# The product with wk as seven block products per batch, with the sums of its blocks streamed from memory

## The chip, the cores and the metric

The kernel runs on one core of one Trainium2 chip. The metric is the device time of one execution in microseconds; the time shown for a kernel is the median of three runs. A profile of one execution comes with it, and the views of that profile are what the prediction reads.

## The reference

Three layers follow each other over 4 batches of 576 tokens with 512 channels: a block-causal attention with 8 heads, a mixer (a token MLP of width 256 and a channel MLP of width 1536), and the layer that the change touches:

```python
x_prev = concat([zeros, x[:, :-1]], axis=1)
xk = mu_k * x + (1 - mu_k) * x_prev
xr = mu_r * x + (1 - mu_r) * x_prev
k = maximum(xk @ w_k, 0)             # w_k: 512 x 1024
v = k * k @ w_v                      # w_v: 1024 x 512
r = 1 / (1 + exp(-(xr @ w_r)))       # w_r: 512 x 512
return r * v
```

Everything is float32 outside. Inside, each operand of a product is split into a high and a low part of a shorter float format, and a product is three matmuls: high by high, high by low, low by high (`dense`, with every matmul recorded at line 214).

## The kernel before

Activations lie channel-major: 128 channels on the partitions, tokens along the free dimension. A batch is cut into two halves of T = 288 tokens, so most matmuls of the last layer are 128 x 128 weights against 128 x 288 tokens.

**Order of the work.** The kernel is not written in the order in which it runs. Each piece of work is registered with `add` (name, engine, an assumed cost, what it depends on, which buffers it takes from rings and frees); `Plan.run` then plays a list schedule over these costs, with priorities that the table `TILT` shifts by kind, and records the instructions in that order. Each engine, and SyncE's queue of DMA issues too, therefore works through a fixed list in order, and an instruction whose inputs are late holds up all that stands behind it on its engine. In the schedule, work on GpSimd and a set of VectorE kinds (`TURNS`) are never placed at the same time.

**Stages.** Attention and the token MLP come first, the channel MLP (`L`: 12 column products per tile of 460 or 464 tokens, `O`: back) follows, then the last layer. TensorE has work in all of them.

**Weights of the last layer.** They arrive as 64-bit words. While the channel MLP runs, each page of 128 x 512 is loaded into one of four staging blocks (`raw`, `rawx`), decoded to float32 in a `td` buffer by two passes on VectorE and one each on ScalarE and GpSimd (`d0` to `d3`), split into high and low (`hi`, `lo`), and written to a scratch array in memory (`pages`). When the channel MLP's own weights are done with, the pages are read back (`ld`): 8 pages of wk and 4 of wr into the 12 slots of ring `w`, those of wv into `w2a` and `w2b`; they stay there for all four batches.

**wk (`K`, before).** Per half batch and per 128 of the 1024 output columns, 12 matmuls of 288 tokens run into one PSUM bank (4 blocks of input channels x 3). ScalarE makes relu of the bank (`KR`, line 974) and VectorE multiplies it with the bank (`KS`, line 978).

**wv (`V`, before and after).** Here the seven-product scheme is in use already. Per batch the squared activations are four blocks B11, B12, B21, B22 (halves of the channels x halves of the tokens), wv is cut in 2 x 2 blocks, and seven products of blocks and of sums of blocks (T1 to T4, line 1017) take the place of eight. The sums of the blocks of wv are made once, in `block_sums` (lines 559 to 595), from pairs of decoded pages: `vs` and `vs2` on VectorE, then the new blocks `vc` and `vd` are split and written like a page. The operands are split per block on ScalarE (`VH`) and VectorE or GpSimd (`VL`, line 211). Each product has two banks of its own, and eight sums per pair of banks (`EV`, line 1038) put the results together in `u`.

**wr (`R`).** Per half batch and 128 output columns 12 matmuls; ScalarE takes the sigmoid (line 994), VectorE multiplies (`Y`, line 998) and SyncE stores 128 x 288. In the schedule `R` waits for the sixth product of `V`.

**Mixing.** xk and xr are made per half batch on ScalarE (`XA`, line 944) and VectorE (`XM`, line 949), and split in 128 x 576 pieces (`XH` line 204, `XL` line 211).

Of the kernel before, what the change touches and what calls it, by code (L numbers as in the profile page):

```python
# [48 lines left out]
TILT = {"ku": -15.8, "h1h": -1.7, "n": -5.4, "h1l": -31.5, "xh": -12.9, "xt": -0.4, "v": 0.1, "k2": 5.6, "q": 9.0, "rc": -20.7, "KH": -1.8, "KL": -2.0, "R": -4.4, "xa": 15.9, "page-v": 16.5, "O": -8.5, "V": -4.8, "Lh": 0.4, "xsh": 17.8, "U": 1.9, "C2": -3.2, "t": -23.3, "xm": -18.3, "K": -4.3, "z": 0.4, "page-c2": 6.1, "page-k": 3.0, "Ll": 4.4, "KS": -6.1, "page-c1": -1.4, "page-t1": -3.0, "xsl": 15.2, "load": 0.5, "L": -8.8, "e": 15.0, "page-r": -3.3, "pv": 0.3, "KR": -21.0, "m": 4.3, "ev": 5.9, "TS": -26.2, "vs": 4.3, "VL": -9.7, "SG": 4.8, "Y": 1.0, "spill": 19.1, "page-vc": 4.1, "page-vd": -7.8, "VH": 3.2, "s": -1.2, "vs2": 4.3, "ld": 13.7, "xl": -2.8, "wr": -5.0, "k1": -4.9, "x2s": 0.8, "x1": 3.7, "mu": -6.1, "om": 9.0, "fetch": -5.1, "page-t2": -0.0}  # L49
# [146 lines left out]
def attn_mixer_rwkv_kernel(ctx: ExitStack, tc: tile.TileContext, z, v, vl, wt1, wt2, wc1, wc2, wk, wv, wr, mu, out):  # L196
# [16 lines left out]
    def mm(o, l, r, start, stop):  # L213
        PE.matmul(o, lhsT=l, rhs=r, start=start, stop=stop)  # L214
# [21 lines left out]
    def c_mm(n):  # L236
        return max(0.108, (n + 32) / 2400)
# [13 lines left out]
    rawt = {"raw": [wp.tile([128, 512], I64, name=f"raw{k}") for k in range(2)]}  # L251
    w1h = tokp.tile([128, 5, DTOK], F32R, name="w1h")
# [231 lines left out]
    plan.ring("td", 3)  # L484
# [21 lines left out]
    def page_ops(name, src, n, room, pri, split_pri=None, gate=(), alloc=(), dense=False, late=False, slack=0.0, store=False):  # L506
# [11 lines left out]
        def pack(e):  # L518
            tl["td", name] = wp.tile([128, 2 * T], U32, tag="td", bufs=3, name="td")[:, 0:c]
            dec2(tl["raw", name], tl["td", name])  # L520

        def hi(e):
            w = room()
            copy(e, w[0], tl["td", name].bitcast(F32))
# [19 lines left out]
    PLACE.update({("v", f): 12 + f for f in range(8)})
    PLACE.update({(nm, j): 20 + 4 * k + j for k, nm in enumerate(("vc", "vd")) for j in range(4)})
    store = nc.dram_tensor("pages", (len(PLACE), 128, 1024), F32).ap()

    def put(name):
        w = tl["raw", name].bitcast(F32)
        w = w[:, 0:512] if name[0] == "vd" else w  # L550
        SP.dma_start(out=store[PLACE[name], :, 0:w.shape[1]], in_=w)


    def block_sums(j, pri):
        a_, b_ = ("v", j), ("v", j + 4)

        def ab():
            return tl["td", a_].bitcast(F32), tl["td", b_].bitcast(F32)

        def vs(e):  # L560
            a, b = ab()
            w = tl["td", ("vc", j)] = wp.tile([128, 2 * T], U32, tag="td", bufs=3, name="td").bitcast(F32)[:, 0:512]
            DVE.tensor_tensor(w[:, 0:256], a[:, 256:512], b[:, 256:512], ALU.add)
            DVE.tensor_tensor(w[:, 256:512], w[:, 0:256], a[:, 0:256], ALU.subtract)

        def vs2(e):
            a, b = ab()
            DVE.tensor_tensor(b[:, 0:256], b[:, 0:256], tl["td", ("vc", j)][:, 256:512], ALU.subtract)
            DVE.tensor_tensor(a[:, 256:512], a[:, 0:256], a[:, 256:512], ALU.subtract)

        add(("vs", j), "DVE", 0.84, [("d3",) + a_, ("d3",) + b_], vs, pri, alloc=[("td", ("td", ("vc", j)))], uses=[("td", a_), ("td", b_)])
        add(("vs2", j), "DVE", 0.84, [("vs", j), ("lo",) + b_], vs2, pri, uses=[("td", a_), ("td", b_), ("td", ("vc", j))])
        for nm, c, ring in (("vc", 512, "raw"), ("vd", 256, "rawx")):
            rk, tk = ("raw", (nm, j)), ("td", (nm, j) if nm == "vc" else b_)

            def src(nm=nm):
                return tl["td", ("vc", j)] if nm == "vc" else ab()[1][:, 0:256]

            def hi(e, nm=nm, c=c, ring=ring, src=src):
                tl["raw", (nm, j)] = rawt[ring][plan.slot[ring, ("raw", (nm, j))]]  # L580
                copy(e, tl["raw", (nm, j)].bitcast(F32R)[:, 0:c], src())

            def lo(e, nm=nm, c=c, src=src):
                w = tl["raw", (nm, j)].bitcast(F32R)
                sub(e, w[:, c:2 * c], src(), f32(w[:, 0:c]))

            add(("hi", nm, j), ("ACT", "POOL"), {"ACT": c_act(c), "POOL": c_pool1(c)}, [("vs2", j)], hi, pri + 0.1, alloc=[(ring, rk)], uses=[tk])
            add(("lo", nm, j), ("DVE", "POOL"), {"DVE": 0.14 + 0.00109 * c, "POOL": c_pool2(c)}, [("hi", nm, j)], lo, pri + 0.1, uses=[rk, tk])
            add(("wr", nm, j), "SP", c_dma(128 * 8 * c), [("lo", nm, j)], lambda e, nm=nm: put((nm, j)), pri, uses=[rk], lat=4.0)
# [116 lines left out]
    plan.ring("w", 12)  # L706
# [6 lines left out]
    pages += [("k", f) for f in range(8)] + [("r", f) for f in range(4)] + [("v", 4 * k + j) for j in range(4) for k in range(2)]  # L713
# [3 lines left out]
    def slot(tag):  # L717
        if tag == "w":
            return wp.tile([128, 2, 512], F32R, tag="w", bufs=12, name="w")
        return pools[tag].tile([128, 2, 512], F32R, tag=tag, bufs=plan.rings[tag], name="w")  # L720

    for nm, f in pages:
        tag = "w" if nm == "c1" else "w2a" if f < 4 else "w2b"
        store_ = nm not in ("c1", "c2")

        def room(nm=nm, f=f, tag=tag, store_=store_):
            if store_:
# [7 lines left out]
        if nm == "v" and f % 4:  # L735
            gate += [("hi", "vd" if f >= 4 else "vc", f % 4 - 1)]
        page_ops((nm, f), wsrc[nm][f], 512, room, when[nm] + (0.5 * f if nm != "v" else f % 4 + f // 4 * 0.5), gate=gate + before,
                 alloc=[] if store_ else [(tag, ("W", nm, f))], dense=nm != "c1" or f >= EARLY,
                 late=nm != "c1" and (f // 4 if nm == "v" else f % 2) == 1, slack=2.0 if nm == "c1" and f < EARLY else 0.0, store=store_)
        if nm == "v" and f >= 4:  # L740
            block_sums(f - 4, when[nm] + f % 4 + 0.5)

    def fetch_page(nm, f, tag):
        if nm == "vd":
            if f == 0:
                tl["vd"] = glob.tile([128, 4, S + 1], F32R, tag="u0", bufs=1, name="vd")
            SP.dma_start(out=f32(tl["vd"][:, f, 0:512]), in_=store[PLACE["vd", f], :, 0:512])
        else:
            t = tl["W", nm, f] = slot(tag)
            SP.dma_start(out=f32(t), in_=store[PLACE[nm, f]].rearrange("p (s c) -> p s c", s=2))  # L750

    back = [("k", f, "w") for f in range(8)] + [("r", f, "w") for f in range(4)] + [("v", f, "w2a") for f in range(4)]
    back += [("vc", f, "w2b") for f in range(4)] + [("v", f, "w2b") for f in range(4, 8)] + [("vd", f, "") for f in range(4)]
    for k, (nm, f, tag) in enumerate(back):
        add(("ld", nm, f), "SP", c_dma(128 * (2048 if nm == "vd" else 4096)), [("wr", nm, f)] + (["spill"] + [("ld", "vd", 0)] * (f > 0) if nm == "vd" else []),
            lambda e, nm=nm, f=f, tag=tag: fetch_page(nm, f, tag), 100.0 + k, alloc=[(tag, ("W", nm, f))] if tag else [], lat=3.0)
# [32 lines left out]
    NGF, NGR = 20, 12  # L789
    plan.ring("gf", NGF)  # L790
    plan.ring("gr", NGR)
    plan.users["raws"] = [("wr", nm, f) for nm in ("v", "vc", "vd") for f in range(8 if nm == "v" else 4)]
    for i in range(2):
        plan.users[f"xhl{i}"] = [("L", max(s for s in range(NX) if s % 2 == i), 11)]
    for i in range(5):
        f = next(f for f in range(7, 12) if (12 * (NX - 1) + f) % 5 == i)
        plan.users[f"hp{i}"] = [("O", NX - 1, f, m) for m in range(4)] if f == 11 else [("O", NX - 1, f)]
    for i in range(NGF):
        if i < 18:
            plan.held.append(("gf", i, "raws" if i < 12 else f"hp{(i - 8) // 2}"))  # L800
    for i in range(NGR):
        plan.held.append(("gr", i, f"xhl{i // 4}" if i < 8 else f"hp{(i - 8) // 2}"))
# [340 lines left out]
```

## Time and profile before

| | |
|---|---|
| time, median of 3 runs | 779.87 us (779.3 to 780.42) |
| profiled execution: its own time, its span | 780.42 us, 778.6 us |
| TensorE busy | 769.7 us, 99% of the span, 5596 matmuls |
| VectorE, ScalarE, GpSimd busy | 483.3, 367.2, 260.6 us |
| mean granted TensorE clock | 0.997 of full speed |
| DMA, over the span | 99 GB/s |

The span runs from the first to the last instruction; the run's own time is 1.8 us more. An engine's busy time is the time in which at least one of its instructions is open; instructions that follow each other directly overlap in these records, so a mean duration is longer than the step from one start to the next.

### The profile page before, as it was taken

The numbers are of one execution on the slowest core, as the hardware profiler recorded it, in microseconds if no ns is written. First come the engines' busy times: TensorE is split into PE (matmuls) and PEld (weight loads), VectorE is DVE, ScalarE is ACT, GpSimd is POOL, SyncE is SP. The second block draws the span as 40 slices with busy tenths as digits, with TensorE's granted clock in tenths as the row PEclk, the third lists the DMA queues.
The fourth block names the chain that finished last, engine by engine and source line by source line (L and its number), as shares of the span: only waits on it lengthen the run. The fifth ranks groups of instructions, "written<-read, shape, count | busy, mean of one in ns | idle before, by whom it ended". The sixth has DMA issues, their size and how long they took to land.

```text
span 778.6 us, 14728 instructions
## 1 busy us (share of the span) xinstructions
PE 769.7 (99%) x5596; PEld 716.7 (92%) x5596; DVE 483.3 (62%) x1245; ACT 367.2 (47%) x902; POOL 260.6 (33%) x352
## 2 busy tenths in 40 slices
PE   9999999999999999999999999999999999999998
PEld 7888899899989888889888888889999999999998
DVE  5898788887475566353326255125866867776782
ACT  5887876767432353141222232023546536545551
POOL 4776676766553466261242112000010010010010
PEclk9999999999999999999999999999999999999999
DMA  7443525221142444516042144447003001001001
GB/s 194 132 123 97 170 82 161 84 89 40 56 122 94 136 136 162 189 55 250 28 162 98 65 162 159 153 168 279 1 8 115 1 1 62 2 1 62 1 1 61
DMA packets 37079, 77.11 MB, mean 99 GB/s; under 512 B 13840, under 2 KB 17936, under 8 KB 37008
## 3 DMA queue, kind: packets, MB, share of 16 engines
q1 hardware_dynamic: 37008, 76.17, 29.4%
q8 instruction: 44, 0.72, 0.4%
q14 instruction: 27, 0.22, 0.1%
HBM read 56.63 MB, written 19.53 MB: 98 GB/s over the span
## 4 chain that ended last, share of the span: by engine, by line
PE 97%; DVE 1%; POOL 0%; ACT 0%; issue 0%; ACTq 0%
PE b L214 69%; PE cd L214 22%; PE b L389 4%; PE b L391 1%; PE b L618 1%; POOL P L380 0%; DVE xnh L206 0%; DVE xnl L636 0%; PE cd L389 0%; DVE pt L206 0%; ACT pt L204 0%; DVE u L1038 0%; DVE td L499 0%; DVE td L500 0%; DVE w L211 0%
## 5 line engine op out<-in xcount | busy, mean ns | idle before, releaser
L214 PE MATMUL b<-xhl,w 128*128 128x288 f32 (+2 forms) x1704 | 287.4, 320 | 0.0
L214 PEld LDWEIGHTS b<-xhl,w 128*128 128x128 f32 x1704 | 261.2, 188 | 11.9
L214 PE MATMUL b<-gx,w 128*128 128x460 f32 (+2 forms) x684 | 149.3, 356 | 0.1
L214 PEld LDWEIGHTS b<-gx,w 128*128 128x128 f32 x684 | 122.2, 188 | 12.3 <-DVE w L211 0.5
L380 POOL TENSOR_SCALAR P<-P,st 128x448 f32<-128x448 f32 (+4 forms) x160 | 84.4, 549 | 50.4 <-DVE st L376 13.0
L214 PE MATMUL cd<-xhl,w 128*128 128x288 f32 (+2 forms) x552 | 97.8, 318 | 0.2 <-DVE u L1038 0.2
L869 ACT ACTIVATE gx<-b 128x460 fp32r<-128x460 f32 (+1 forms) x46 | 25.5, 555 | 147.5 <-PE b L214 147.5
L371 ACT ACTIVATE P<-P,st 128x576 f32<-128x576 f32 (+4 forms) x160 | 88.4, 557 | 13.0 <-DVE st L366 12.8
L872 DVE SCALAR_TENSOR_TENSOR gx<-b,gx 128x460 fp32r<-128x460 f32 (+1 forms) x46 | 29.3, 636 | 103.7 <-ACT gx L869 103.6
L214 PEld LDWEIGHTS cd<-xhl,w 128*128 128x128 f32 x552 | 85.8, 188 | 4.0 <-DVE u L1038 0.4
L504 POOL TENSOR_TENSOR td<-td,raw 128x512 int32<-128x512 int32 (+2 forms) x37 | 44.8, 1210 | 91.2 <-DVE td L500 71.4
L214 PE MATMUL cd<-gx,w 128*128 128x460 f32 (+2 forms) x228 | 56.6, 356 | 0.2 <-DVE u L1038 0.2
L214 PE MATMUL b<-z 64*128 64x224 f32 (+3 forms) x320 | 54.0, 356 | 0.0
L211 POOL TENSOR_TENSOR xhl<-raw,xhl 128x288 fp32r<-128x288 f32 x9 | 7.3, 816 | 133.7 <-ACT xhl L204 133.7
L366 DVE CUSTOM_DVE_ANT_0 P<-b,mask 128x448 f32<-128x448 f32 (+3 forms) x128 | 48.9, 416 | 2.7 <-PE b L214 1.9
L389 PE MATMUL b<-ident,P 128*128 128x128 f32 x310 | 47.8, 278 | 0.4 <-DVE pt L206 0.4
L214 PEld LDWEIGHTS b<-z 64*128 64x128 f32 x320 | 44.3, 186 | 4.1 <-issue 1.0
L214 PEld LDWEIGHTS cd<-gx,w 128*128 128x128 f32 x228 | 41.0, 188 | 4.2 <-DVE u L1038 0.4
L214 PE MATMUL b<-pt,vs 128*64 128x128 f32 x600 | 41.9, 275 | 0.0
L204 ACT COPY pt<-b 128x448 f32<-128x448 f32 (+1 forms) x55 | 29.8, 559 | 23.4 <-PE b L389 13.3
L214 PE MATMUL cd<-z 64*128 64x288 f32 x128 | 39.0, 424 | 0.0
L389 PEld LDWEIGHTS b<-ident,P 128*128 128x128 f32 x310 | 34.8, 141 | 4.3 <-issue 0.7
(193 smaller groups left out, 1253.4 us busy)
## 6 DMA issues: line engine op xcount, KB each, us to landing
w<-pages SPq DMA_DIRECT2D x24, 512.0 KB, 5.2
z<-in_z SPq DMA_DIRECT2D x16, 576.0 KB, 3.9
raw<-in_wc SPq DMA_DIRECT2D x18, 512.0 KB, 3.7
pages<-raw SPq DMA_DIRECT2D x14, 512.0 KB, 2.9
pages<-rawx SPq DMA_DIRECT2D x10, 512.0 KB, 2.6
out<-u SPq DMA_DIRECT2D x32, 144.0 KB, 1.8
vs<-in_v SPq DMA_DIRECT2D x16, 256.0 KB, 3.6
rawx<-in_wc SPq DMA_DIRECT2D x6, 512.0 KB, 4.5
```

The costliest lines, as they stand in the source:

```text
L204: ACT.copy(o, i)
L211: (DVE if e == "DVE" else POOL).tensor_tensor(o, a, b, ALU.subtract)
L214: PE.matmul(o, lhsT=l, rhs=r, start=start, stop=stop)
L366: DVE.tensor_tensor_reduce(p_view(p, h, i), s_view(p, h, i), m, -0.125, 3.0e38, ALU.add, ALU.min, tl["st", p, h][:, 0, i:i + 1])
L371: ACT.activation(w, w, ACTF.Exp, bias=st[:, 0, i:i + 1], scale=-1.0, accum_out=st[:, 1, i:i + 1])
L380: POOL.tensor_scalar(w, w, tl["st", p, h][:, 2, i:i + 1], 1.0, ALU.mult, ALU.mult)
L389: PE.transpose(t[:, o + 128 * k:o + 128 * k + 128], tl["P", p, i][:, c:c + 128], ident)
L391: PE.transpose(t[:, 64 * k:64 * k + 128], tl["P", p, i][:, 128 * i:128 * i + 128], ident)
L504: POOL.tensor_tensor(td.bitcast(I32), td.bitcast(I32), lw, ALU.add)
L618: PE.transpose(t[0:rows, 256 * k + 128 * p:256 * k + 128 * p + 128], u[b][:, 2 * g + p, c:c + rows], ident)
L869: ACT.activation(tl["h", t, f][0], tl["lb", t, f][:, 0:w], ACTF.Relu)
L872: DVE.scalar_tensor_tensor(tl["h", t, f][1], tl["lb", t, f][:, 0:w], 0.0, f32(tl["h", t, f][0]), ALU.max, ALU.subtract)
```

## The change

- wk is cut into 2 x 2 blocks (256 input channels x 512 output columns) and xk into four blocks per batch (256 channels x 288 tokens). Seven products of blocks take the place of eight. A product (`K, i, n`) is four PSUM banks of six matmuls.
- A product that belongs to several results is not added up by VectorE from banks of its own: banks stay open over several products (`INTO`). ScalarE copies the partial sum out between two of them (`s1`, `u2`, `u4`), TensorE goes on in the same bank after that copy, and VectorE adds the bank of another product to the copy (`c11`, `c22`, `c21`). The same scheme replaces the eight sums of `V`.
- The sums of the blocks of xk are made per batch (`XT`, 4 of 128 x 576), the sums of the blocks of wk once, by `block_sums`, from 4 pairs of pages; with wv there are 8 pairs instead of 4. The scratch array holds 28 units of seven products and 4 pages of wr.
- Ring `w` has 8 slots (was 12). The 14 units of wk and the 4 pages of wr are read from the scratch array anew for every batch, 18 x 512 KB. The other 4 slots (`wx`) become float32 buffers. The operand splits of xk and xr go through four slots (`xop`); rings `td`, `gf`, `gr` are larger (6, 29, 14 for 3, 20, 12), the added `td` slots being the staging blocks once all pages are written.
- `R` now waits for the last product of `K` and not for `V`. The assumed DMA costs of the schedule are lower (a page load 2.1 + 4.0 for 3.1 + 6.0 us, a write 2.1 + 2.0 for 3.1 + 4.0), and `TILT` has new values for all kinds.

```diff
-    plan.ring("td", 3)
+    plan.ring("td", 6)
+    plan.held += [("td", i, "raws") for i in (3, 4, 5)]
...
-        add(("l",) + name, "SP", c_dma(r * c * 8), list(gate) + ["begin"], load, pri, alloc=[(ring, rk)], lat=6.0 + slack)
+        add(("l",) + name, "SP", r * c * 8 / 250e3 if dense else c_dma(r * c * 8), list(gate) + ["begin"], load, pri, alloc=[(ring, rk)], lat=4.0 if dense else 6.0 + slack)
...
+    SETS = [("k", q, 2, 4 * q) for q in range(2)] + [("v", 0, 4, 0)]
+    PAIRS = [(nm, q, j, o + j, o + J + j) for nm, q, J, o in SETS for j in range(J)]
...
-    plan.ring("w", 12)
+    plan.ring("w", 8)
+    plan.ring("wx", 4)
...
-    pages += [("k", f) for f in range(8)] + [("r", f) for f in range(4)] + [("v", 4 * k + j) for j in range(4) for k in range(2)]
+    pages += [(nm, x) for nm, _, _, *ab in PAIRS[:4] for x in ab] + [("r", f) for f in range(4)] + [(nm, x) for nm, _, _, *ab in PAIRS[4:] for x in ab]
...
+    for i in range(B):
+        for n in range(7):
+            for q in range(2):
+                name = ("ld", "k", i, q, n)
+                fetch_op(name, last + made_in("k", q, n, 0), ("W", "k", i, q, n), ("k", q, n, 0), "w", None if i == 0 else 130.0 + 16 * i - 9 + 0.1 * n)
+                last = [name]
+        for f in range(4):
+            name = ("ld", "r", i, f)
+            fetch_op(name, last + [("wr", "r", f)], ("W", "r", i, f), ("r", f), "w", None if i == 0 else 130.0 + 16 * i - 8)
+            last = [name]
...
+    OPS = ("B11", "B21", "T2", "T3", "T1", "B22", "T4")
+    TSUM = (("T1", "B12", "B11"), ("T2", "B22", "T1"), ("T3", "B22", "B12"), ("T4", "B21", "T2"))
+    INTO = (0, 1, 0, 2, 0, 0, 2)
...
+                after = [("xt", i, "T2")] if g else [("xm", i - 1, 1, y) for y in ("B11", "B21", "B12", "B22")] if i else [("L", NX - 2, 0), ("hi", "vd", len(PAIRS) - 1)]
+                add(ak, "ACT", 1.06, need[c] + after, XA, px, alloc=[("td", ak)])
...
+                    if n in (0, 1, 3):
+                        tl[bk] = bank(bk)
+                    w = ("W", "k", i, f // 2, n)
+                    o = tl["xo", i, 0, x]
+                    dense(tl[bk], [unit(w, j, f % 2) for j in range(2)], [(o[:, 0, j], o[:, 1, j]) for j in range(2)], n in (0, 1, 3), True, more=True)
...
+                hold = {2: [("s1", i, f)], 4: [("u2", i, f)], 5: [("u4", i, f)], 6: [("c22", i, f)]}.get(n, [])
...
+            for name, n, x in (("s1", 0, "B11"), ("u2", 2, "B21"), ("u4", 4, "B22"), ("kr", 5, "B12")):
+                kout(name, "ACT", c_act(T), [("K", i, n, f)], lambda e, s=snap, x=x, name=name: s(e, x=x, fn=ACTF.Relu if name == "kr" else ACTF.Copy), x, f, True, [0])
+            for name, n, x, y, old in (("c11", 1, "B11", 1, "s1"), ("c22", 3, "B22", 2, "u4"), ("c21", 6, "B21", 2, "u2")):
+                kout(name, "DVE", c_dve(T), [("K", i, n, f), (old, i, f)], lambda e, p=plus, x=x, y=y: p(e, x=x, y=y), x, f, False, [y])
+                add(("KS", i, x, f), "DVE", c_dve(T), [(name, i, f)], lambda e, s=square, x=x: s(e, x=x), P0 - 5, uses=[("op", i, x, f)])
+            add(("KS", i, "B12", f), "DVE", c_dve(T), [("kr", i, f)], lambda e, s=square12: s(e), P0 - 5, uses=[("op", i, "B12", f), ("kb", i, 0, f)])
...
+                prev = ("R", i, m - 1, c) if m else ("R", i, 3, 0) if c else ("K", i, 6, 3)
...
+                hold = {2: "s1", 4: "u2", 5: "u4", 6: "c22"}.get(n)
+                hold = [("ev", i, hold, m) for m in ms] if hold and 0 in js else []
...
+            for x, n, r, c in (("s1", 0, 0, 0), ("u2", 2, 1, 0), ("u4", 4, 1, 1)):
+                add(("ev", i, x, m), "ACT", c_act(T), [("V", i, n, 2 * m + 1 if n == 4 else 3)] + mixed, lambda e, f=vsnap, r=r, c=c: f(e, r=r, c=c), P0 - 8, uses=[("vb", i, 0, m)])
+            for x, n, r, c, y, old in (("c11", 1, 0, 0, 1, "s1"), ("c22", 3, 1, 1, 2, "u4"), ("c21", 6, 1, 0, 2, "u2")):
+                add(("ev", i, x, m), "DVE", c_dve(T), [("V", i, n, 3), ("ev", i, old, m)], lambda e, f=vplus, r=r, c=c, y=y: f(e, r=r, c=c, y=y), P0 - 8, uses=[("vb", i, y, m)])
```

## Rows read from the trace of the kernel before

**Rows 1.** The page's head: the span, and busy time per engine.

```profile
span 778.6 us, 14728 instructions
PE 769.7 (99%) x5596; PEld 716.7 (92%) x5596; DVE 483.3 (62%) x1245; ACT 367.2 (47%) x902; POOL 260.6 (33%) x352
```

**Rows 2.** Windows by stage: window, its length, busy us (count) per engine, clock, DMA.

```profile
0.00:214.00 214.00, 210.84 (x2240) 190.43 (x2241) 164.57 (x605) 150.73 (x446) 142.73 (x239) 1.00 0.38 112
...
531.00:775.00 244.00, 243.68 (x1826) 242.96 (x1824) 173.28 (x390) 128.39 (x300) 18.70 (x23) 1.00 0.10 37
775.00:778.60 3.60, 0.05 (x1) 0.00 (x0) 0.46 (x1) 0.41 (x1) 0.00 (x0) 0.90 0.23 82
```

**Rows 3.** Timeline of TensorE and ScalarE in wk: start, length, engine, line, operation, [idle before].

```profile
532.93 0.41 ACT L974 ACTIVATE gx<-b 128x288 f32<-128x288 f32 x1 [8.09 <-PE b L214]
...
534.34 3.36 PE L214 MATMUL b<-xhl,w 128*128 128x288 f32 x24
...
537.54 1.76 PE L214 MATMUL cd<-xhl,w 128*128 128x288 f32 x12
```

**Rows 4.** Waits of TensorE from 530 us to the end: total us, times, longest.

```profile
PE cd L214 <- DVE u L1038: 0.3, 2, 0.2
```

**Rows 5.** Groups of VectorE instructions, 531 to 775 us: busy, mean ns.

```profile
L211 DVE TENSOR_TENSOR xhl<-td,xhl 128x576 fp32r<-128x576 f32 x28 | 21.2, 756 | 6.1 <-ACT xhl L204 6.1
L1038 DVE TENSOR_TENSOR u<-b,u 128x288 f32<-128x288 f32 x42 | 18.1, 452 | 7.5 <-PE b L214 7.5
```

**Rows 6.** Timeline of VectorE in the second batch.

```profile
612.65 1.80 DVE L949 SCALAR_TENSOR_TENSOR td<-u,mu_sb,td 128x288 f32<-128x288 f32 x4
...
617.40 1.01 DVE L1017 TENSOR_TENSOR raw<-rawx,raw 128x288 f32<-128x288 f32 x1
...
622.62 0.75 DVE L211 TENSOR_TENSOR xhl<-td,xhl 128x576 fp32r<-128x576 f32 x1
623.29 0.82 DVE L211 TENSOR_TENSOR xhl<-gx,xhl 128x288 fp32r<-128x288 f32 x2
```

**Rows 7.** Timeline of GpSimd over the same stretch.

```profile
617.28 0.81 POOL L211 TENSOR_TENSOR xhl<-gx,xhl 128x288 fp32r<-128x288 f32 x1 [16.25 <-ACT xhl L204]
```

**Rows 8.** Timeline of SyncE's DMA issues: first wk page, wv pairs, last page writes.

```profile
280.06 0.33 SPq L516 DMA_DIRECT2D raw<-in_wk  x1
...
357.91 1.18 SPq L516 DMA_DIRECT2D raw<-in_wv  x1
...
396.89 0.33 SPq L516 DMA_DIRECT2D raw<-in_wv  x1
...
456.33 0.33 SPq L516 DMA_DIRECT2D raw<-in_wv  x1
...
484.37 0.66 SPq L551 DMA_DIRECT2D pages<-rawx  x1
```

**Rows 9.** Timeline of one wv pair: its first decode and its last split.

```profile
413.37 0.66 ACT L495 ACTIVATE raw<-raw 128x512 int32<-128x512 uint32 x1
...
424.00 0.42 DVE L211 TENSOR_TENSOR rawx<-td,rawx 128x256 fp32r<-128x256 f32 x1
```

**Rows 10.** DMA issues: count, KB each, median us to landing; then minimum, median, maximum for the scratch array.

```profile
w<-pages SPq DMA_DIRECT2D x24, 512.0 KB, 5.2
raw<-in_wv SPq DMA_DIRECT2D x4, 512.0 KB, 5.2
...
DMA to landing us min/median/max: 2.6/3.6/11.1
```

**Rows 11.** Windows, columns as in rows 2: an idle of TensorE, and a full DMA stretch.

```profile
215.00:220.00 5.00, 3.46 (x28) 3.19 (x26) 4.74 (x10) 1.77 (x4) 3.29 (x4) 1.00 0.54 168
220.00:225.00 5.00, 4.73 (x26) 4.73 (x27) 3.39 (x8) 1.52 (x3) 2.37 (x2) 0.66 0.09 34
520.00:540.00 20.00, 20.00 (x121) 18.75 (x120) 10.67 (x21) 8.28 (x19) 0.55 (x1) 1.00 0.84 328
```

More of the change, by code (lines that the diff above doesn't have):

```diff
@@ L549, in put, with halves, block_sums @@
         w = tl["raw", name].bitcast(F32)
[L550 to L555, printed above, removed]
+        if name in PLACE:
+            SP.dma_start(out=store[PLACE[name]], in_=w)
+            return
+        n, k = PAIR[name] if name in PAIR else (name[1], name[0])
+        nm, q, j = PAIRS[n][:3]
+        for a, x in enumerate(PARTS[k]):
+            o = 512 * (j % 2)
+            SP.dma_start(out=store[PLACE[nm, q, x, j // 2], :, o:o + 512], in_=w[:, 512 * a:512 * a + 512])
+    def halves(w):
+        return w.bitcast(F32R).rearrange("p (a h c) -> p h a c", h=2, c=256)
+    def block_sums(n, pri):
+        nm_, q_, j_, ia, ib = PAIRS[n]
+        a_, b_ = (nm_, ia), (nm_, ib)
         def ab():
@@ L573, in block_sums @@
+        add(("vs2", n), "DVE", 0.84, [("vs", n), ("lo",) + b_], vs2, pri, uses=[("td", a_), ("td", b_), ("td", ("vc", n))])
         for nm, c, ring in (("vc", 512, "raw"), ("vd", 256, "rawx")):
[L574 to L589, printed above, removed]
+            rk, tk = ("raw", (nm, n)), ("td", (nm, n) if nm == "vc" else b_)
@@ L752, in attn_mixer_rwkv_kernel @@
[L752 to L756, printed above, removed]
+                 late=nm != "c1" and (k if (nm, f) in PAIR else f % 2) == 1, slack=2.0 if nm == "c1" and f < EARLY else 0.0, store=store_)
@@ new lines, in attn_mixer_rwkv_kernel, with made_in, fetch_unit @@
+        if k:
+            block_sums(n, when[nm] + n % 4 + 0.5)
+    def made_in(nm, q, n, jp):
+        k = {x: k for k, xs in PARTS.items() for x in xs}[n]
+        got = []
+        for m, (a, b, j, *ab) in enumerate(PAIRS):
+            if (a, b, j // 2) == (nm, q, jp):
+                got.append(("wr", k, m) if k in ("vc", "vd") else ("wr", nm, ab[k]))
+        return got
+    def fetch_unit(key, place, tag):
+        t = tl[key] = slot(tag)
+        SP.dma_start(out=f32(t), in_=store[PLACE[place]].rearrange("p (s c) -> p s c", s=2))
@@ L797, in attn_mixer_rwkv_kernel, with slab, third @@
         plan.users[f"hp{i}"] = [("O", NX - 1, f, m) for m in range(4)] if f == 11 else [("O", NX - 1, f)]
[L798 to L802, printed above, removed]
-    def gx(i, w, dt):
-        return pools["xp"].tile([128, w], dt, tag=f"gx{i}", bufs=1, name=f"gx{i}")
+    for i in range(27):
+        plan.held.append(("gf", i, "raws" if i < 6 else f"wx{(i - 6) // 3}" if i < 18 else f"hp{(i - 12) // 3}"))
+    for i in range(14):
+        plan.held.append(("gr", i, f"xhl{i // 4}" if i < 8 else f"hp{(i - 8) // 3}"))
+    for i in range(4):
+        plan.held.append(("xop", i, f"xhl{1 - i // 2}"))
+    def slab(i):
+        return pools["xp"].tile([128, 2 * XW], F32R, tag=f"hp{i}", bufs=1, name=f"hp{i}")
+    def third(key, make, k):
+        if key not in tl:
+            tl[key] = make()
+        return tl[key][:, T * k:T * k + T]
     def g32(key, dt=F32):
@@ L933, in attn_mixer_rwkv_kernel, with home_of, unit, both @@
+    HOME = {"T1": "B11", "T3": "B12", "T4": "B21"}
+    FIRST = {"T1": "B11", "T4": "B21"}
+    INTO = (0, 1, 0, 2, 0, 0, 2)
+    def home_of(x):
+        return HOME.get(x, x)
+    def unit(key, j, c):
+        w = tl[key][:, j]
+        return w[:, 128 * c:128 * c + 128], w[:, 256 + 128 * c:384 + 128 * c]
+    def both(f, o, x):
+        return o(f, x)
+    for i in range(B):
         b = order[i]
         ub = home[b]
-        p0 = 130.0 + 16 * i + 3 * c
-        us, pr = slice(1 + T * c, 1 + T * c + T), slice(T * c, T * c + T)
```

413 lines of the change are left out of this document (225 added, 188 removed).

## The prediction

> **What bounds the kernel now.** I read the page's head first: TensorE is open for 769.7 of 778.6 us [rows 1]. A busy share alone says little, so the windows by stage came next. In the last layer (531 to 775 us) TensorE shows 243.68 of 244.00 us with 1826 matmuls, two of them left over from the stage before, at full clock [rows 2]. The timeline shows what full means there: 24 matmuls of 288 tokens start at 534.34 and the next begins at 537.54, so one step is 3.20 / 24 = 0.1333 us [rows 3], and 1824 x 0.1333 = 243.2 us is the whole stage. The list of waits has only 0.3 us in two waits [rows 4]. So this stage is as long as its number of matmuls, and a matmul removed is worth 0.133 us, as long as something else does not become late. VectorE is open for 173.28 us of the same 244 [rows 2]; that is the engine to watch. The DMA engines are nearly idle there (0.10).
>
> **What the change removes.** Before, wk takes 2 halves x 8 columns x 12 = 192 matmuls a batch, 768 in all. After, it takes 7 products x 4 banks x 6 = 168 a batch, 672 in all, of the same shape. wv and wr keep theirs (168 and 96). Removed: 96 x 0.1333 = 12.8 us, all on the path that sets the end. A batch goes from 456 x 0.1333 = 60.8 to 432 x 0.1333 = 57.6 us.
>
> **What it adds on VectorE.** The real price of an instruction is the step from one start to the next: two of 288 in 0.82 us with 0.45 the length of one make a step of 0.37; a 128 x 576 split steps 623.29 - 622.62 = 0.67; a mixing instruction 1.80 / 4 = 0.45 [rows 6]. Before, a batch has 82 instructions of 288 (16 squares, 16 sums T, 28 low parts, 14 sums of banks, 8 products with r), 16 of mixing and 8 splits, with the few that GpSimd takes counted in: 30.3 + 7.2 + 5.4 = 42.9 us of 60.8. After: 12 sums of wk's banks come, 8 of wv's sums go to ScalarE or vanish (86 x 0.37 = 31.8), 3 more splits and 4 sums of xk (15 x 0.67 = 10.1), mixing 7.2: 49.1 us of 57.6, or 85% for 71%. The tight part is from the start of wk's seventh product to the next batch: 288 matmuls, 38.4 us, in which VectorE has 66 of 288, some 6 splits, 2 sums of xk and 8 mixings: 24.4 + 4.0 + 1.3 + 3.6 = 33.4 us. It fits, so I cost these instructions at nothing, with TensorE's own matmuls as cover; without the cover see the first rival. ScalarE has 128.39 us in this stage [rows 2], 32 a batch; three more splits and four more copies add about 4.
>
> **What the open banks add.** TensorE may go on in a bank only after ScalarE's copy. The copy of the first bank takes 0.41 us and starts at once when TensorE is through with it (the ACT row of [rows 3]). Between the end of a partial sum and the next matmul in its bank lie at least three other groups of six for wk (2.4 us) and 12 matmuls for wv (1.6 us). A copy fits unless ScalarE's queue holds something late. No row shows such a wait; from below it is 0, from above it is one idle like that at 215 us, where TensorE lost 5.00 - 3.46 = 1.5 us, 0.3 more in the next 5 us, and then ran those at a granted clock of 0.66 of full speed, the lower level for part of it, another 1.7 us [rows 11]: 3.5 us each, 14 for four batches. The nearest row is rather the one of the same stage, 0.15 us a wait [rows 4]. With more such places than before (banks, copies, four operand slots) I take 0.4 us a batch, 1.6 in all.
>
> **What the streaming adds.** 18 loads of 512 KB a batch are 9.4 MB in 57.6 us, 164 GB/s on queues that are idle now; 520 to 540 us ran at 328 [rows 11]. A load lands 5.2 us after its issue by the median [rows 10]. A pair of slots comes free when a product is through, and its next unit is needed three products later, 3 x 24 x 0.1333 = 9.6 us. Hidden, so 0. The out stores and loads share SyncE's list, which is why a late store could hold up loads (third rival).
>
> **What is moved: the pages.** wk's pages now go in pairs like wv's. In the channel MLP, before, the first wk page is issued at 280.06, wv's four pairs follow from 357.91, and the last write goes out at 484.37 [rows 8]. The 12 single pages took 77.9 us, 6.5 each. Two pairs took 456.33 - 396.89 = 59.4 us, 29.7 each. The instructions of one pair span 413.37 to 424.42, 11.1 us [rows 9]; the rest is the load, the write and the assumed time of both in the schedule, which falls by 3.0 us each for load and write. With 29.7 - 6 = 23.7 us eight pairs and four pages take 189.6 + 26 = 216 us: done near 496, 35 us before wk begins. So 0, with the channel MLP as cover. The order of wr ahead of wv in the last batch moves the tail: instead of a sigmoid and a product (0.41 and 0.46 us, the last window of [rows 2]) two sums and two products on VectorE stand between the last matmul and the last store, 3 x 0.37 + 0.46 = 1.6 for 0.9: +0.6 us. The tilted priorities reorder the first 214 us too, where TensorE idles 3.2 us [rows 2]: 0, with 1.5 either way.
>
> **The sum.** Against the profiled execution's 780.42 (span 778.6 and 1.8 around it): -12.8 + 1.6 + 0.6 = -10.6, so 769.8. That execution lies 0.55 above the median of 779.87, so the forecast is **769.3 us**.
>
> **Rivals.** *VectorE becomes the bound.* If an instruction costs its whole length, because each waits for the one before (0.452 for 288, 0.756 for a split [rows 5], and for mixing the longer spacing of 0.51, my estimate from these), the tight part is 29.8 + 4.5 + 1.5 + 4.1 = 40.0 us against 38.4: 1.6 us late a batch, 6.4 in all, **775.7**. For it: a sum with two inputs from SBUF took 1.01 us instead of 0.45 while GpSimd worked from 617.28 to 618.09 [rows 6, 7], and 12 squares a batch change from reading PSUM to reading SBUF only. Against it: where VectorE had work queued it did step by 0.37. The Trainium skill (SBUF — State Buffer, Who interferes with whom) says that a VectorE instruction with two SBUF inputs and a GpSimd instruction that reads SBUF exclude each other for the whole instruction; the 1.01 us row agrees, and by that rule the 12 squares join those that can be held up.
>
> *The pages come too late (the other side).* wk's operands wait for the last pair (`hi`, `vd`, 7). If pairs keep their 29.7 us, because decode and splits stand in lists between relus that wait for TensorE, eight pairs and four pages end at 280.06 + 237.6 + 26 = 543.7 and the first operand some 4 us later (two mixings on each of two engines and a split): wk starts near 547.7 instead of 531, 16.7 us late, some of it saved by pages that start earlier. I take 13 us and 2 for the clock, as in rows 11: 769.3 + 15 = **784**. It decides from a pair time of (531 - 4 - 26 - 280) / 8 = 27.6 us; above 27.6 + 10 / 8 = 28.9 nothing is left of the gain. For it: the order is fixed in advance, and pairs did take 29.7. Against it: load and write are assumed shorter now, and they do land in 5.2 and 3.6 us [rows 10].
>
> *The weights stream too late.* If a load lands in 11.1 us, the longest seen [rows 10], the fifth product of a batch waits 11.1 - 9.6 = 1.5 us, and once late it stays late: with half of the clock's loss 1.7 a batch, 6.8 in all, **776**. For it: during wk a product eats 1 MB in 3.2 us, 328 GB/s, exactly the most of [rows 11]. Against it: eight units are there in advance.
>
> **How the numbers follow.** Forecast 0.64 (its own range 766 to 773: no stall at all is 767.7, the first 214 us 1.5 either way; 1 us more stall a batch is 773), VectorE 0.15, streaming 0.09, pages 0.12. What a measurement can tell from no change is 0.2%, 1.6 us: faster is under 778.3, slower over 781.4. All of the forecast's case, 0.12 of VectorE's, and 0.06 of the stream's lie under 778.3, with the few of the pages' case that are only 10 us late near it: 0.82. Slower: 0.10 of the pages and 0.03 of the others, 0.13. Between: 0.05. The range that holds it 8 times in 10 goes from 766.0 (0.04 below) to 778.5 (0.16 above).
>
> **What would show it.** Right: 1728 matmuls of 288 from about 531 us on, in some 230 us, steps of 0.1333; TensorE's waits there below 3 us in all; VectorE between 80 and 90% busy there; the DMA share up, with no wait of TensorE on `w`; the last page write before 527. Wrong: TensorE waiting for `xop` operands or for low parts of 288 (VectorE), for `w` (stream), one long idle and a granted clock below 1 before the first product of wk (pages), or repeated idles of 1.5 us with the clock at its lower level after each. More than 10.6 us lost in all of these and the change is no gain; a first stage longer by more than 2 us would also break the sum.

## The result, and the profile after

The changed kernel takes **766.01 us** (median of 4 runs, 765.42 to 766.2), the kernel before 779.76 (4 runs): 0.9822 of it, 95% interval 0.9805 to 0.9839. The gain is 13.8 us where 10.6 were forecast (779.87 to 769.3), and 766.0 lies on the lower edge of the range. The profiled execution takes 766.2 us, 14.2 less than that of before.

The head of the page of the changed kernel, answering to [rows 1]:

```profile
span 764.4 us, 14828 instructions
PE 756.0 (99%) x5500; PEld 702.7 (92%) x5500; DVE 528.9 (69%) x1283; ACT 380.4 (50%) x936; POOL 308.3 (40%) x384
```

96 matmuls fewer, TensorE's share the same; VectorE rose from 62% to 69%. To see where the time went, the span is cut where the last layer begins. The timeline of TensorE in the changed kernel, first and last group of the layer, and the list of its waits from 520 us on (total us, times, longest):

```profile
527.49 0.96 PE L214 MATMUL b<-xhl,w 128*128 128x288 f32 x6
...
759.16 0.96 PE L214 MATMUL b<-xhl,w 128*128 128x288 f32 x6
...
PE cd L214 <- DVE u L1203: 0.2, 1, 0.2
PE cd L214 <- DVE wg L1103: 0.2, 1, 0.2
```

| part of the span | before | after | difference | forecast |
|---|---|---|---|---|
| up to the first matmul of the last layer | 531.13 | 527.49 | -3.64 | 0, 1.5 either way |
| last layer, first matmul to the end of the last | 243.9 | 232.6 | -11.3 | -12.8 + 1.6 |
| from there to the end of the span | 3.6 | 4.3 | +0.7 | +0.6 |

(Before, the last matmul ends near 775.05 and ScalarE starts on its bank at 775.09.) So the layer that the change rebuilds did what was worked out, to 0.1 us. What the sum lacks lies in front of it.

The windows of the changed kernel by stage, columns as in [rows 2]. Behind them the stretch that answers to the idle of [rows 11], of TensorE alone: window, its length, busy us (count), granted clock, DMA share, GB/s.

```profile
0.00:214.00 214.00, 210.49 (x2237) 190.04 (x2238) 163.65 (x605) 151.89 (x448) 140.03 (x238) 1.00 0.39 112
214.00:531.00 317.00, 317.00 (x1564) 285.94 (x1564) 174.66 (x277) 92.89 (x170) 115.69 (x103) 1.00 0.44 152
531.00:764.40 233.40, 228.51 (x1703) 226.70 (x1702) 190.61 (x402) 135.65 (x320) 52.59 (x44) 1.00 0.49 170
...
210.00:215.00 5.00, 4.45 (x36) 1.00 0.00 0
215.00:220.00 5.00, 5.00 (x42) 1.00 0.59 176
220.00:225.00 5.00, 5.00 (x36) 1.00 0.08 34
```

From 214 to 531 us TensorE is without a gap now. Before, it had a wait of 1.8 us there. This is VectorE and TensorE of the kernel before around that wait, and windows of TensorE alone behind it:

```profile
218.69 0.43 DVE L499 TENSOR_SCALAR td<-rawx 128x512 uint32<-128x512 uint32 x1
219.15 0.69 DVE L500 SCALAR_TENSOR_TENSOR td<-rawx,td 128x512 uint32<-128x512 uint32 x1
219.76 0.45 DVE L692 TENSOR_TENSOR u<-cd,u 128x288 f32<-128x288 f32 x1
...
220.27 0.40 PE L214 MATMUL cd<-w2h,h1h 128*128 128x288 f32 x1 [1.82 <-DVE u L692]
...
221.50:222.00 0.50, 0.50 (x5) 0.51 0.00 0
224.50:225.00 0.50, 0.50 (x4) 0.57 0.00 0
225.00:225.50 0.50, 0.50 (x6) 1.00 0.00 0
```

TensorE wants a bank of the token MLP, and the sum that empties it (L692) stands behind the decoding of a page (L499, L500) in VectorE's list. 1.2 us after TensorE resumes, its clock is granted at 0.50, the lower of its two levels, until about 224.9. That is 1.8 us of idle and half of some 3.4 us at that level, 3.5 in all. It accounts for the early start: both kernels have 3772 matmuls ahead of the last layer, and with the matmuls of the two traces numbered in order the changed kernel is 0.3 us behind at the 2266th (217 us) and 3.2 us ahead at the 2302nd (225 us in the kernel before). What is gained and lost elsewhere ahead of the layer adds up to 0.1 us. In the changed kernel the same sums (L726) stand ahead of the decoding:

```profile
210.47 1.19 DVE L726 TENSOR_TENSOR u<-b,u 128x288 f32<-128x288 f32 x3
212.27 0.46 DVE L726 TENSOR_TENSOR u<-cd,u 128x288 f32<-128x288 f32 x1 [0.61 <-PE cd L214]
212.64 0.42 DVE L509 TENSOR_SCALAR td<-raw 128x512 uint32<-128x512 uint32 x1
```

What stays there is a wait of 0.6 us with no loss of clock. So the order of VectorE's list at this one place was redrawn; the experiments ask which part of the change did that.

### The profile page after: what moved, and what is told of

The parts are those of the page before. It is cut to its first block, busy times and chain, and to the rows that moved or that the text cites. A ratio compares the mean times of both kernels' runs of the same rounds, so it can differ in the third digit from the quotient of the medians.

```text
span 764.4 us, 14828 instructions
## 1 busy us (share of the span) xinstructions
PE 756.0 (99%) x5500; PEld 702.7 (92%) x5500; DVE 528.9 (69%) x1283; ACT 380.4 (50%) x936; POOL 308.3 (40%) x384
## 4 chain that ended last, share of the span: by engine, by line
PE 97%; DVE 1%; ACT 1%; POOL 1%; issue 0%; DVEq 0%
PE b L214 69%; PE cd L214 21%; PE b L390 5%; PE b L652 1%; PE b L392 1%; POOL P L381 1%; DVE raw L1042 0%; DVE wg L1103 0%; DVE u L1203 0%; DVE pt L206 0%; PE cd L390 0%; ACT xhl L204 0%; ACT pt L204 0%; ACT wg L1100 0%; DVE xnh L206 0%
## 5 line engine op out<-in xcount | busy, mean ns | idle before, releaser
L214 PE MATMUL b<-xhl,w 128*128 128x288 f32 (+2 forms) x1581 | 270.9, 322 | 0.0
L214 PEld LDWEIGHTS b<-xhl,w 128*128 128x128 f32 x1581 | 245.0, 188 | 11.8
L214 PE MATMUL b<-hp,w 128*128 128x460 f32 (+2 forms) x735 | 156.5, 351 | 0.0
L214 PEld LDWEIGHTS b<-hp,w 128*128 128x128 f32 x735 | 129.3, 188 | 11.8
L372 ACT ACTIVATE P<-P,st 128x576 f32<-128x576 f32 (+4 forms) x160 | 88.4, 557 | 13.8 <-DVE st L367 13.5
L214 PEld LDWEIGHTS cd<-xhl,w 128*128 128x128 f32 x513 | 80.7, 188 | 4.7 <-DVE wg L1103 0.4
L956 ACT ACTIVATE hp<-b 128x460 fp32r<-128x460 f32 (+1 forms) x46 | 25.5, 555 | 112.6 <-PE b L214 110.7
L959 DVE SCALAR_TENSOR_TENSOR hp<-b,hp 128x460 fp32r<-128x460 f32 (+1 forms) x46 | 29.2, 635 | 62.5 <-ACT hp L956 62.5
L214 PE MATMUL cd<-hp,w 128*128 128x460 f32 (+2 forms) x243 | 58.7, 353 | 0.2 <-DVE u L1203 0.2
L214 PEld LDWEIGHTS cd<-hp,w 128*128 128x128 f32 x243 | 43.2, 188 | 4.5 <-DVE u L1203 0.4
L959 DVE SCALAR_TENSOR_TENSOR hp<-cd,hp 128x460 fp32r<-128x460 f32 (+1 forms) x14 | 8.9, 636 | 41.9 <-ACT hp L956 41.9
```

What stands on the lines that cost most here:

```text
L214: PE.matmul(o, lhsT=l, rhs=r, start=start, stop=stop, skip_group_check=more)
L372: ACT.activation(w, w, ACTF.Exp, bias=st[:, 0, i:i + 1], scale=-1.0, accum_out=st[:, 1, i:i + 1])
L956: ACT.activation(tl["h", t, f][0], tl["lb", t, f][:, 0:w], ACTF.Relu)
L959: DVE.scalar_tensor_tensor(tl["h", t, f][1], tl["lb", t, f][:, 0:w], 0.0, f32(tl["h", t, f][0]), ALU.max, ALU.subtract)
```

## The experiments

Two questions: what removed the wait ahead of the last layer, and are the three things that were costed at nothing (VectorE's added work, the streaming, the pages) covered as well as the prediction said. The ratio given with each is to the kernel before, with its interval.

**The wait in front: assumed costs or priorities.** First the kernel before with one ingredient of the new schedule each.

```diff
-        add(("l",) + name, "SP", c_dma(r * c * 8), ..., lat=6.0 + slack)
+        add(("l",) + name, "SP", r * c * 8 / 250e3 if dense else c_dma(r * c * 8), ..., lat=4.0 if dense else 6.0 + slack)
-            add(("wr",) + name, "SP", c_dma(128 * 4096), ..., lat=4.0)
+            add(("wr",) + name, "SP", 2.1, ..., lat=2.0)
```

> The kernel before, with the new kernel's assumed costs of page loads and page writes in the schedule and nothing else. Theory A (the 3.6 us by which the last layer starts earlier come from the order around 214 us, which the assumed load cost sets): the 1.8 us wait of TensorE behind the sums of the token MLP is gone, the first matmul of wk starts near 528 us instead of 531.1, the time is about 776.5, 3 us under the kernel before. Rival B (the priorities do it): 779.8, within 0.8 of the kernel before, wait still there. Rival C (it takes the pairs of wk pages): also 779.8.

Measured: 782.46 us, 1.0029 (1.0019 to 1.004). The wait behind L692 is 0.3 us, TensorE is at full clock, and the last layer starts early; but new waits appear in that layer (TensorE's waits in this run, then its first group there):

```profile
PE b L214 <- DVE gx L211: 0.9, 2, 0.5
PE b L214 <- DVE xhl L211: 0.9, 1, 0.9
...
PE cd L214 <- DVE u L692: 0.3, 1, 0.3
...
527.70 1.76 PE L214 MATMUL b<-xhl,w 128*128 128x288 f32 x12
```

Theory A holds for the start (527.70 for 531.13) and fails for the time: the layer takes 249 us instead of 243.9 (its last group of 12 starts at 775.00 and lasts 1.76). That the old priorities do not fit the order which the new costs make is a reading; no run of the kernel before has the new costs and the new priorities together. Rival C is out for the start, since this kernel has no pairs of wk pages.

```diff
-TILT = {"ku": -15.8, "h1h": -1.7, "n": -5.4, ...}
+TILT = {"ku": -19.4, "h1h": -6.6, "n": -5.5, ...}   # new values for the kinds of the kernel before
```

> The kernel before, with the new kernel's priorities for all kinds that it has, and the old assumed costs. Theory A: the wait near 216 us stays, 779 to 782. Rival B: the wait is gone, 776.5. Rival C: 779 to 782 as well.

Measured: 780.84 us, 1.0007 (0.9998 to 1.0016). The wait behind L692 and the first group of the last layer in this run:

```profile
PE cd L214 <- DVE u L692: 0.6, 1, 0.6
...
528.81 3.36 PE L214 MATMUL b<-xhl,w 128*128 128x288 f32 x24
```

The layer starts 2.3 us earlier and takes 246.7 us, 2.8 more than before, so the time misses rival B's 776.5. For the start B is as right as A: the priorities alone remove the long wait too. It came from one place in one order, and both new orders have another.

**The same in the changed kernel, and the late pages.**

```diff
-        ... "SP", r * c * 8 / 250e3 if dense else c_dma(r * c * 8), ... lat=4.0 if dense else 6.0 + slack)
+        ... "SP", c_dma(r * c * 8), ... lat=6.0 + slack)
-            ... "SP", 2.1, ... lat=2.0)      # and 0.0041 * c for the blocks vc, vd
+            ... "SP", c_dma(128 * 4096), ... lat=4.0)
```

> The new kernel with the old assumed costs of page loads and writes. Theory A: the wait near 216 us comes back, the last layer starts 3 us later, 769. Rival B or C: no such wait, 766. The rival of the prediction on late pages: pairs keep 29.7 us, eight of them end after 527 us, TensorE idles some 13 us ahead of wk and the time is 780 or more, which would also hide the 3 us.

Measured: 783.27 us, 1.004 (1.0028 to 1.0053), 17.3 us over the changed kernel. Longest waits of TensorE, one of them in the channel MLP, a window with all engines (columns as in [rows 2]) and one of TensorE alone, and SyncE's first and last page issues in this run:

```profile
PE cd L214 <- ACT xhl L204: 4.2, 1, 4.2
PE cd L214 <- POOL w L208: 2.9, 2, 2.1
PE cd L214 <- DVE xhl L211: 2.0, 1, 2.0
...
279.51 0.68 PE L214 MATMUL cd<-hp,w 128*128 128x460 f32 x2 [2.08 <-POOL w L208]
...
540.00:545.00 5.00, 0.61 (x1) 0.29 (x1) 5.00 (x12) 3.17 (x7) 1.31 (x1) 0.65 0.85 290
545.00:550.00 5.00, 3.92 (x16) 0.50 0.47 188
...
281.79 0.33 SPq L526 DMA_DIRECT2D raw<-in_wk  x1
...
529.69 0.57 SPq L578 DMA_DIRECT2D pages<-rawx  x1
```

This is the kind of loss that the prediction's rival on late pages names, though not as it priced it. The last page is written at 529.69. TensorE begins wk at 531.73, stands still for 4.2 and 2.0 us between 539 and 546 us while operands of wk are made (VectorE is busy in all of 540 to 545), and runs at its lower clock until about 551.7. The layer takes 245.4 us, 12.8 more than in the changed kernel. The other 4.2 us are lost ahead of it: from 271 to 281 us TensorE waits for weights of the channel MLP itself (2.08 us at 279.51, with no fall of its clock behind it), which no rival had. With the new costs the same eight pairs run from 273.22 to 481.18:

```profile
273.22 0.33 SPq L526 DMA_DIRECT2D raw<-in_wk  x1
...
481.18 0.89 SPq L578 DMA_DIRECT2D pages<-rawx  x1
```

The edit changes assumed costs alone; what differs is the list in which each engine works, packed closer with the new ones. The wait of the token MLP is 0.6 us in the run with the old costs, not 1.8: theory A, that the new costs are needed to remove it, is refuted in this kernel, where the new priorities suffice.

```diff
+TILT.update({"ku": -15.8, "h1h": -1.7, "n": -5.4, ...})   # old values for all kinds that the kernel before had
```

> The new kernel with the old priorities for all kinds that the kernel before had; the new kinds keep theirs. Theory A: no wait near 216 us, the last layer starts near 527.5 us as in the new kernel, and the last layer loses up to 4 us to an order that was not made for it: 766 to 770. Rival B: the last layer starts 3 us later, 769 to 773.

Measured: 767.21 us, 0.9833 (0.982 to 0.9847); the layer starts at 528.36. As A expected. The wait of the token MLP is 0.3 us here, so the new costs suffice too. The new priorities are worth about 1 us at most; the two intervals overlap.

**What a matmul is worth.**

```diff
+        for _ in range(again):                       # 2 in the opening groups of wk
+            mm(t[:, 0:w], ws[0][0], xs[0][0], True, False, more)
```

> The new kernel with 96 matmuls of 288 tokens put back: the first matmul of each opening group of wk (12 groups a batch) is issued three times instead of once, each time clearing the bank, so the result does not change. Theory (the last layer is as long as its matmuls): +12.8 us, 778.8. Rival (part of the gain is not the matmuls, because TensorE has hidden waits in the last layer that added matmuls would fill): less than +10, under 776.

Measured: 777.98 us, 0.9979 (0.997 to 0.9989): +12.0. The layer takes 244.7 us for 232.6, 0.125 us for each of the 96. The theory holds and the rival (under +10) does not. Of the 0.8 us that are missing, some 0.3 are stalls that became shorter; the rest is not explained.

**wr behind wv.**

```diff
-                prev = ... else ("K", i, 6, 3)
+                prev = ... else ("V", i, 5, 3)
```

> The new kernel with the products with wr behind the sixth product with wv again, as before. Theory (wr fills the time in which the second wv operand is made from wk's last product, and frees the operand slots for the next batch): 1 to 4 us more, 767 to 770, with waits of TensorE behind low parts (line 211) right after wk's last product. Rival (the order of wr is worth nothing, wv's first product covers the chain alone): within 0.8 us of 766.0.

Measured: 787.5 us, 1.0107 (1.0088 to 1.0125), 21.5 us over the changed kernel. The waits of TensorE, its timeline and clock behind the first batch's wk, then VectorE and GpSimd at that place:

```profile
PE b L214 <- DVE hp L211: 11.4, 6, 4.2
...
555.57 0.94 PE L214 MATMUL b<-hp,w 128*128 128x288 f32 x5 [2.26 <-DVE hp L211]
...
557.00:562.00 5.00, 4.76 (x23) 0.66 0.02 3
...
551.99 1.68 DVE L1156 TENSOR_TENSOR wg<-wg,raw 128x288 f32<-128x288 f32 x1
...
555.07 0.45 DVE L211 TENSOR_TENSOR hp<-rawx,hp 128x288 fp32r<-128x288 f32 x1
...
551.71 1.65 POOL L211 TENSOR_TENSOR xhl<-td,xhl 128x576 fp32r<-128x576 f32 x1
```

The direction is the theory's, the size is over five times the most that it gave. Behind wk's last product the second operand of wv has to be summed, squared and split (sums T stand in the list ahead of it, one of them held up to 1.68 us beside a GpSimd piece), and with wr gone TensorE has nothing to do. Each of the four batches has such an idle, of 1.9 to 4.2 us, and the clock falls to 0.50 at each. The reordering of wr, which reads like a detail of the change, is worth more in this kernel than the removed matmuls. The priorities were not chosen anew for this order; how much of the loss other priorities would win back is not shown.

**VectorE's cover.**

```diff
-                    sub(e, tl["vl", i, x, j], tl["op", i, x, j], f32(tl["vh", i, x, j]))
+                    for _ in range(2 if e == "DVE" and j < 2 else 1):
+                        sub(e, tl["vl", i, x, j], tl["op", i, x, j], f32(tl["vh", i, x, j]))
```

> The new kernel, in which VectorE makes the low parts of wv's operands for two of the four pieces twice over (some 10 more instructions of 288 a batch, 3.7 us by the step of 0.37; the schedule does not know of it). Theory of the prediction (33.4 of 38.4 us in the tight part, so 5 us of cover a batch): under 1.5 us more, below 767.5. Rival (VectorE is at its bound already): all of it shows, 12 us or more, 778.

Measured: 779.47 us, 0.9992 (0.9983 to 1.0002): +13.5. There were 53 more instructions on VectorE, 13 a batch and not 10, and its busy time from 527 us on rose from 191.9 to 216.9, 0.47 each. Two writes of the same piece last 0.94 us together (569.37 below), two of different pieces 0.82 [rows 6]. So 24.9 us were added, not 15, and 11.4 of them (2.9 a batch) hidden. TensorE's waits in the layer rose by 8.8 us; most of the other 4.7 is the lower clock behind two of them. Counting the waits alone, 4.0 a batch are hidden. Neither expectation is met as written; 5 us of cover a batch would have hidden 20. The longest wait shows the mechanism, TensorE, VectorE and GpSimd:

```profile
569.50 0.67 PE L214 MATMUL cd<-hp,w 128*128 128x288 f32 x3 [2.81 <-DVE u L1204]
...
566.82 2.26 DVE L211 TENSOR_TENSOR xhl<-wg,xhl 128x288 fp32r<-128x288 f32 x2
569.00 0.44 DVE L1204 TENSOR_TENSOR u<-cd,u 128x288 f32<-128x288 f32 x1
569.37 0.94 DVE L211 TENSOR_TENSOR xhl<-ge,xhl 128x288 fp32r<-128x288 f32 x2
...
567.15 1.61 POOL L211 TENSOR_TENSOR xhl<-rawx,xhl 128x576 fp32r<-128x576 f32 x1
```

Two low parts of 0.45 us take 2.26 us beside a GpSimd piece, and the sum that frees a bank stands behind them.

**The stream's margin.**

```diff
+        if tag == "w":
+            SP.dma_start(out=extra[len(copied)], in_=store[PLACE[place], :, 0:512])
```

> The new kernel with a copy of 256 KB from memory to memory ahead of each of the 72 loads of wk's units and wr's pages, so that the streams move half as much again. Theory (eight units in advance cover the loads): under 1 us more, below 767. Rival (the stream has no margin, since it fills the queues to 0.95 for 28 us a batch): 2 us or more a batch late, 774 and above, with waits of TensorE on w.

Measured: 773.94 us, 0.9922 (0.9902 to 0.9942): +7.9. TensorE's wait in this run, then a window of TensorE alone in the changed kernel itself:

```profile
PE b L214 <- DMA w<-pages: 6.5, 6, 1.4
...
642.50:647.50 5.00, 5.00 (x40) 1.00 0.98 347
```

The rival is nearer (2 us a batch, and waits on `w`). In the changed kernel the queues run at about 0.9 and more for 20 to 30 us of each batch; 18 loads at 339 GB/s take 28. Half as much traffic again is not hidden. Smaller additions were not tried.

**Who should do the small pieces.**

```diff
-                add(("VL", i, x, j), ("DVE", "POOL"), c_tt2, ...)        # also XT, XSL, TS
+                add(("VL", i, x, j), "DVE", 0.46, ...)
```

> The new kernel in which only VectorE may do the sums T, the sums of xk and the low parts of the last layer (GpSimd did 44 of them); the schedule is made anew with that. Theory (GpSimd and VectorE exclude each other, so GpSimd's help there costs VectorE as much as it saves): squares and mixings fall back to 0.45 and 0.51 us by the mean, VectorE's busy time stays within 8 us of 192, the time within 3 us of 766.0. Rival (VectorE is at its bound and needs the help): 44 x 0.37 = 16 us more on VectorE, 12 us or more in the time, 778, as the added low parts did.

Measured: 776.71 us, 0.9958 (0.9945 to 0.9972): +10.7. The largest group of squares (L1107) and TensorE's waits in this run; then, of the changed kernel, the largest groups of mixings and squares, and a GpSimd piece with the VectorE instructions beside it:

```profile
L1107 DVE SCALAR_TENSOR_TENSOR wg<-wg 128x288 f32<-128x288 f32 x24 | 10.3, 451 | 0.0
PE b L214 <- ACT hp L204: 3.3, 5, 1.1
PE b L214 <- DVE hp L211: 3.2, 6, 1.1
```

```profile
L1042 DVE SCALAR_TENSOR_TENSOR td<-u,mu_sb,td 128x288 f32<-128x288 f32 x28 | 18.8, 715 | 0.1
...
L1107 DVE SCALAR_TENSOR_TENSOR wg<-wg 128x288 f32<-128x288 f32 x22 | 13.5, 641 | 0.0
...
550.46 1.64 POOL L211 TENSOR_TENSOR xhl<-raw,xhl 128x576 fp32r<-128x576 f32 x1
...
550.74 0.45 DVE L1103 TENSOR_TENSOR rawx<-b,rawx 128x288 f32<-128x288 f32 x1
551.10 1.31 DVE L1107 SCALAR_TENSOR_TENSOR rawx<-rawx 128x288 f32<-128x288 f32 x1
```

On VectorE the theory holds: these squares fall from 0.641 to 0.451 us (all 48 of the line from 0.594 to 0.450), and VectorE's busy time is 193.8 instead of 191.4 us though it does 44 pieces more. The rows from 550.46 on show which instructions are held up: the sum L1103 reads one input from a bank and takes its 0.45 us beside GpSimd, the square L1107 reads both from SBUF and takes 1.31. In the whole layer 23 such sums and 13 such squares meet a GpSimd piece; the longest sum takes 0.46 us, the squares 0.99 by the mean, and the 35 squares that meet none 0.45. On the time the theory fails: 776.71 where it allowed 769. TensorE's waits (6.5 us on ScalarE's and VectorE's split pieces of wv's operands) point to the operands behind wk, which come later without GpSimd. The order was drawn anew with priorities that were chosen for the other one; what part of the 10.7 us that costs is not shown.

```diff
-    TURNS = {"rc", "d2", "vs", "lo", "xm", "xsl", "Y", "TS", "VL"}
+    TURNS = {"rc", "d2", "vs", "lo", "xm", "xsl", "Y", "TS", "VL", "KS", "xt"}
```

> The new kernel, where the schedule keeps the squares and the sums of xk, both with two inputs from SBUF, out of GpSimd's time as it does the other such kinds. Theory (they are held up beside GpSimd now: squares take 0.64 by the mean instead of 0.45): squares fall to 0.45, GpSimd gets fewer pieces, the short waits of TensorE in the last layer shrink, 764 to 766. Rival (the order is worth more than the lock): 766 to 769.

Measured: 776.63 us, 0.9957 (0.9944 to 0.9969). Squares at 0.449, GpSimd down to 12 pieces, the same loss. Theory and rival both missed the size, and the same doubt about the order applies.

```diff
-    c_tt2 = {"DVE": 0.46, "POOL": 0.86}
+    c_tt2 = {"DVE": 0.39, "POOL": 0.86}
```

> The new kernel with 0.39 instead of 0.46 us as the assumed VectorE cost of the sums T and the low parts, near the step of 0.37 that the trace shows. Theory (the assumed cost only sets the order, and the order has little left to give): 765 to 768. Rival (a truer cost gives a better order): 763 to 765.

Measured: 764.84 us (764.45 to 765.53), 0.9808 (0.9795 to 0.9821): the fastest median here, 1.2 us under the changed kernel, with intervals that overlap. It lies on the rival's side by the number alone; that it is a gain is not shown.

```diff
-                add(("xm",) + ak[1:], "DVE", 1.04, ...
+                add(("xm",) + ak[1:], "DVE", 0.92, ...        # and 0.68 for 0.76 of XT and XSL
```

> As the version with 0.39 us for sums T and low parts, and the assumed VectorE costs of the 128 x 576 pieces (0.68 instead of 0.76) and of a mixing (0.92 instead of 1.04 for two) near their steps as well. Theory (the order has little left to give; TensorE's stage is 230.4 us of matmuls and 231.4 with its last waits): 764 to 766. Rival (the schedule needs the reserve of the longer costs, since a piece beside GpSimd takes longer than its step): 767 and above.

Measured: 767.48 us, 0.9843 (0.9829 to 0.9856). The rival's side (767 and above): truer costs all round did not give a better order.

## Why the prediction was right or wrong

*What bounds the kernel, and the removal: right.* The layer is its matmuls; 1728 x 0.1333 = 230.4 of 232.6 us, and putting 96 back gave +12.0 of 12.8. The waits, VectorE's share (191.4 of 232.6 us, 82%) and the last page write (482) came out as its signs of being right.

*Stalls in the last layer: right in size.* 232.6 - 230.4 = 2.2 us are lost, 0.7 before, so +1.5 for the 1.6 taken. They are six places of 0.3 to 0.4 us. The row of the same stage was the right one to lean on for this term; the idle at 215 us was not. None of the experiments tells how much of it the open banks cause.

*The tail: right*, +0.7 for +0.6.

*The first stages: wrong, and this is the step that failed.* The prediction put it "0, with 1.5 either way", by the 3.2 us of idle in the first 214 us, and left the start of the last layer where it was. The last layer starts 3.64 us earlier. In those 214 us TensorE idles 3.5 us now for 3.2 before. The idle that could go was not there; it was the one of [rows 11], 3.5 us with the clock that it cost, which the prediction had priced and used only as an upper bound for something else. A new order of the same stage redraws that idle too: two other orders of the kernel before lost it as well (starts at 527.70 and 528.81). The sum should have carried the chance of -3.5, and the lower end of the range should have been 764. That 766.0 lies just within the range as given is luck: nothing in it allowed for this.

*The pages: right.* 23.7 us a pair and an end near 496 were worked out; the four pairs of wv took (481.18 - 383.06) / 4 = 24.5, and the earlier start, at 273.22, brings the end to 482. The side on which late pages fall was right too. That the run with the old costs took 783.27 for the rival's 784 is luck in good part: its pairs took (529.69 - 281.79 - 26) / 8 = 27.7 us, only just over the 27.6 from which the rival starts to cost, yet the layer lost 12.8 us, and 4.2 more were lost in the channel MLP, which the rival does not have.

*VectorE "costed at nothing, it fits": right for this kernel, with a reason that holds only in part.* The cover is some 3 to 4 us a batch, not 5. The price of 0.37 does not hold for an instruction with two SBUF inputs beside a GpSimd piece; what the first rival feared is there (the largest group of mixings at 0.715 us, of squares at 0.641, up to 1.7 for one). The lock that the Trainium skill describes (SBUF — State Buffer, Who interferes with whom) agrees with these rows, with the sums from a bank that stay at 0.45, and with 0.451 where GpSimd is kept out. Yet VectorE's busy time decides nothing by itself: the changed kernel and the versions with fewer GpSimd pieces, with VectorE busy for 190 to 194 us, differ by 10.7 us.

*Streaming "hidden, so 0": right*, but without the margin that 164 GB/s on average suggests. The rival's 1.7 us a batch does not follow from its terms (1.5 and half of the clock's 1.7 are 2.35); the run with half as much traffic again lost 2.0.

## What to carry to other kernels

When a kernel's order is computed anew, every idle of the bound engine that comes from the order, anywhere in the span, is in play, with the clock that it may cost: list those idles first and put each into the range. A margin read from averages (busy share, GB/s over a batch) says little where work is fixed in lists; look at the one place where the chain is longest, and at what the bound engine has to do meanwhile. Here that filler, wr between wk and wv, was worth 21.5 us, more than the 96 matmuls saved.

## What the runs showed of the hardware that was not expected

In the kernel before, an idle of 1.8 us was followed by TensorE's clock at 0.50, 1.2 us after it had resumed and for some 3.4 us. An idle of that length does not always cost the clock: in the changed kernel with the old assumed costs one of 2.08 us, at 279.51, was not followed by a fall, and of 54 executions of the kernel before, 12 show a mean granted clock of 1.000 (779.2 to 779.5 us) where 37 show 0.997 (779.5 to 780.6). This suggests that a part of the 3.5 us is not lost in each execution.

A VectorE instruction of 0.45 us with two SBUF inputs lasted up to 1.7 us beside a GpSimd piece of 128 x 576, which takes 1.6 us; one that reads a bank was not held up. And two VectorE writes of the same piece took 0.94 us together, two of different pieces 0.82.
